# Other ranks, limits and planned durations for the list scheduler of a kernel with attention and a two-layer network

## The chip, the core and the metric

The kernel runs on one core of one Trainium2 chip. The metric is the time of one execution in microseconds (us) of the device. The engines of the core are called as in the profile: PE multiplies matrices (PEld loads its weights), DVE, ACT and POOL work on elements, and SP issues the loads and stores. Each engine takes its own instructions strictly in the order in which the program lists them; semaphores make one engine wait for another. PSUM, where PE writes, has 8 banks of 128 x 512 float32.

## The reference

The inputs are q, k and v of shape (8, 8, 576, 64) in float32 and two weight matrices, 512 x 2048 and 2048 x 512, which arrive as 8-byte floats. Keys and values are averaged over groups of 8 positions before the attention; its result is the input of a two-layer network with an activation made of softplus and erf.

```python
k_p = k.reshape(B, H, Sp, pool, D).mean(axis=3)
v_p = v.reshape(B, H, Sp, pool, D).mean(axis=3)
scores = scale * np.matmul(q, k_p.transpose(0, 1, 3, 2))
scores = scores - np.max(scores, axis=-1, keepdims=True)
attn = np.exp(scores)
attn = attn / (np.sum(attn, axis=-1, keepdims=True) + 1e-09)
x = np.matmul(attn, v_p)            # then heads side by side: 4608 tokens x 512
...
h = x @ w_in
sp = np.maximum(h, 0.0) + np.log1p(np.exp(-np.abs(h)))
g = h * erf(sp)
return (g @ w_out).astype(np.float32)
```

## The kernel before, in words

**Precision.** PE multiplies in a format with fewer bits than float32, so each operand is split into a high part and a remainder, and each product is made of three matmuls (high x high, low x high, high x low). That is why ACT (or POOL) casts, and DVE or POOL subtracts, after nearly every step.

**Chunks and steps.** The 4608 tokens are cut into 9 chunks (`ck`) of 512. For each chunk there are 16 steps (`ft`), one for each 128 columns of `w_in` and 128 rows of `w_out`: 144 steps `n` in all. The first product of a step (`gemm1`, L584) is 12 matmuls into one bank of kind `h`; the second (`gemm2`, L631) is 12 matmuls that add to four banks of kind `o`, which belong to the chunk until they are stored (L643 to L649). `pair(n)` takes two steps together: softplus (L602) and erf (L609) need different tables of ACT, loaded once each for a pair. Then come the product (L612), the cast `gh` (L614) and the remainder `gl` (L617). In chunk 0 (`kept` is false) the two `h` banks are held until the product is done; later the first product is copied out at once (L589, L590).

**Attention.** `job` treats a block of up to 256 tokens of one batch. A batch's first block loads the keys and values (L383), sums them over 8 positions (L386 on DVE for the first two batches, L389 to L393 on POOL for the others), and writes the split keys `kbd` (L402, L404) and values `vah`, `val`, `vb` (L412 to L425). `softmax_tile` treats 128 tokens: load and split q (L436 to L442), scores on PE (L476, in the wide form L452 and L454), the maximum (L481), in chunk 0 its scaling (L484), the exponentials on ACT (L491, L501), the sum, its guard (L505), the reciprocal (L507), the small product `bb` on POOL (L513), the normalisation (L517), transposes (L524, L531), and the split of the result (L528, L529, L536, L538, L541). Then PE multiplies with the values (L561), and ACT and DVE split the result into `xh` and `xl` (L565, L567), the input of `gemm1`. A chunk's `gemm1` needs all attention of that chunk.

**Weights.** There are 32 pieces (16 of each matrix), 512 KB each. `load_weights` loads one (L345) and turns its 8-byte floats into a high and a low part: two operations of ACT (L348, and L353 or on POOL L355), two of DVE (L357, L359), a cast on ACT or POOL (L309, L310) and a subtraction on POOL (L364). It uses one of the two buffers `f`, one of the three `hs`, and a bank of kind `cv`. All this happens once, in chunk 0.

**The order.** The program does not run in the order in which it is written. `op` records each operation with its engine, a planned duration, and a rank (`prio`, smaller is sooner) in units of steps: `gemm1` of step n has rank n, `gemm2` n + `G2`. `Program.order` then plays the whole kernel through with these durations and lists the operations. For each engine it takes, among the operations whose inputs are ready and whose rank is at most `window` above what PE has reached, the one with the smallest planned start plus `SLACK` nanoseconds for each unit of rank; of the engines' choices the earliest start goes first. An operation with two possible engines may go to its second one where that ends no more than `BIAS` later. `DELAY` is the planned time from one engine's end to another's start, `SAME` that within an engine, `DGE` and the start value of `free["SP"]` belong to the loads. `port` marks DVE operations that the plan keeps apart from POOL. The buffers of each kind, and the banks by kind (`CAP_H`, `CAP_O`, `CAP_ATT`, `CAP_CV`, eight together), limit what may be under way. Where PE is planned to be idle before `FILL` (57 us), fillers are put in (L675): matmuls on constants whose result nobody reads. The list is fixed when the program is built; at run time nothing is reordered.

The ranks that matter here: a weight piece has the rank `due` = ft + `W_IN`, or ft + `G2` + `W_OUT`; its load has `due` - `LEAD`, its conversion `due` - 3 to `due` - 2.4. The tiles of chunk 0 have `T0` + `T0_STEP` x (0 to 3); those of a later chunk 16 x (ck - 1) + 4 x t less `SHIFT` (or `B1` for chunk 1). Keys are summed at the rank of their batch's first tile plus `KEYS`, values at that plus `VALS`; a load stands one rank ahead of its sum. The values' matmuls come `VAL_R` after the last tile of the block.

## Time and profile before

| what | us |
|---|---|
| median of 3 runs | 950.01 (949.89 to 951.83) |
| the profiled execution, its own time | 949.92 |
| its span (first to last instruction) | 948.0 |
| PE busy in the span | 928.0 (98%) |
| ACT, DVE, POOL busy | 653.7, 531.9, 348.0 |
| all loads of weights, keys, values and q of chunks 0 and 1 | DMA above 0.8 busy until about 70 us |

The profile comes from one execution. A row of a timeline gives the start in us from the beginning of the span, the length, the engine, the line of the kernel, the operation, what it writes and reads, how many were merged, and in brackets the engine's idle time before it with what ended that. A row of a view by stretches gives the stretch, its length and the busy time (and number of instructions) of each engine in it. The end of a matmul is modelled, so neighbouring matmuls overlap in the rows; distances between starts are better read than lengths.

### The profile page before, as it was taken

How to read it: one execution, taken by the hardware profiler on the slowest of the kernel's cores; microseconds unless marked ns; L12 is line 12 of the kernel's file. 1: busy time of each engine (PE TensorE's matmuls, PEld its weight loads, DVE VectorE, ACT ScalarE, POOL GpSimd, SP SyncE). 2: the span in 40 equal slices, each digit the busy share in tenths (PEclk: the TensorE clock that was granted, in tenths of full speed). 3: DMA queues.
4: the chain of work that ended last, by engine and by line, in shares of the span. 5: the costliest groups of instructions: out<-in, count | busy, mean ns of one | idle time of the engine just before them, and what ended most of it. 6: DMA issues, size and time to landing. Idle time of an engine off the chain costs nothing.

```text
span 948.0 us, 13049 instructions
## 1 busy us (share of the span) xinstructions
PE 928.0 (98%) x4636; PEld 771.9 (81%) x4636; DVE 531.9 (56%) x1021; ACT 653.7 (69%) x1131; POOL 348.0 (37%) x451
## 2 busy tenths in 40 slices
PE   7899989999999999999999999999999999999998
PEld 6778868888888888888888888888888888888886
DVE  6978686755565454555565655655476446423232
ACT  4789985867676767766676667766676667656664
POOL 3689986243322354235321452234342111101000
PEclk9999999999999999999999999999999999999999
DMA  8990112212111121111110122002210010001001
GB/s 322 363 357 7 37 36 70 77 38 62 39 45 36 38 67 45 45 43 47 51 67 13 37 68 78 23 14 59 68 56 23 1 45 1 1 1 44 1 1 45
DMA packets 30352, 58.58 MB, mean 62 GB/s; under 512 B 7120, under 2 KB 7248, under 8 KB 30288
## 3 DMA queue, kind: packets, MB, share of 16 engines
q1 hardware_dynamic: 30000, 57.23, 18.1%
q8 instruction: 37, 0.61, 0.3%
q10 hardware_dynamic: 288, 0.52, 0.1%
q14 instruction: 27, 0.22, 0.1%
HBM read 48.30 MB, written 9.44 MB: 61 GB/s over the span
## 4 chain that ended last, share of the span: by engine, by line
PE 84%; DVE 1%; ACT 0%; POOL 0%; issue 0%; POOLq 0%
PE banks L631 38%; PE banks L584 37%; PE banks L561 4%; PE banks L452 2%; PE banks L524 1%; PE banks L454 1%; PE banks L476 1%; PE banks L531 0%; DVE kbd L404 0%; DVE z L503 0%; ACT L501 0%; DVE hs L612 0%; ACT y L602 0%; DVE z L505 0%; DVE s L517 0%; ACT s L501 0%
## 5 line engine op out<-in xcount | busy, mean ns | idle before, releaser
L584 PE MATMUL banks<-xh,wi 128*128 128x512 f32 x1152 | 381.2, 393 | 3.5 <-DVE y L612 2.8
L631 PE MATMUL banks<-wo,gh 128*128 128x512 f32 x1152 | 363.2, 396 | 0.8 <-DVE etl L529 0.7
L584 PEld LDWEIGHTS banks<-xh,wi 128*128 128x128 f32 x1152 | 217.1, 188 | 51.1 <-DVE y L612 4.4
L631 PEld LDWEIGHTS banks<-wo,gh 128*128 128x128 f32 x1152 | 207.5, 188 | 39.6 <-DVE etl L529 1.1
L631 PE MATMUL banks<-wo,gl 128*128 128x512 f32 x576 | 225.3, 391 | 0.0
L584 PE MATMUL banks<-xl,wi 128*128 128x512 f32 x576 | 225.1, 391 | 0.0
L617 DVE TENSOR_TENSOR gl<-hs,gh 128x512 fp32r<-128x512 f32 x73 | 53.6, 736 | 157.4 <-ACT gh L614 153.3
L617 POOL TENSOR_TENSOR gl<-hs,gh 128x512 fp32r<-128x512 f32 x55 | 71.4, 1298 | 175.2 <-ACT gh L614 174.6
L631 PEld LDWEIGHTS banks<-wo,gl 128*128 128x128 f32 x576 | 108.1, 188 | 24.2 <-DVE gl L617 0.4
L590 ACT COPY hs<-banks 128x512 f32<-128x512 f32 x56 | 32.8, 586 | 136.2 <-PE banks L584 133.3
L584 PEld LDWEIGHTS banks<-xl,wi 128*128 128x128 f32 x576 | 108.6, 188 | 21.8
L614 ACT CAST gh<-hs 128x512 fp32r<-128x512 f32 x128 | 78.4, 614 | 35.5 <-PE banks L631 31.3
L589 DVE COPY hs<-banks 128x512 f32<-128x512 f32 x72 | 49.8, 692 | 92.1 <-PE banks L584 91.7
L602 ACT ACT_TABLE_LOAD x72 | 92.4, 1283 | 3.0 <-DVE gl L617 1.8
L612 DVE TENSOR_TENSOR hs<-y,hs 128x512 f32<-128x512 f32 x128 | 84.1, 697 | 15.2 <-ACT y L609 15.1
L609 ACT ACT_TABLE_LOAD x68 | 87.2, 1283 | 1.2
L442 POOL TENSOR_TENSOR ql<-raw,qh 128x512 fp32r<-128x512 f32 (+1 forms) x36 | 44.4, 1232 | 106.4 <-ACT qh L309 106.2
L609 ACT ACTIVATE y<-y 128x1024 f32<-128x1024 f32 (+1 forms) x73 | 76.4, 1048 | 0.8
L389 POOL TENSOR_TENSOR raw<-raw 128x256 f32<-128x256 f32 (+1 forms) x60 | 50.9, 849 | 70.5 <-DMA raw<-vl 40.8
L602 ACT ACTIVATE y<-hs 128x512 f32<-128x512 f32 x128 | 73.8, 624 | 0.7
L541 POOL TENSOR_SCALAR etb<-etb 32x256 fp32r<-32x256 f32 (+1 forms) x40 | 18.3, 458 | 88.8 <-ACT etb L536 54.8
L501 ACT ACTIVATE s<-s,cst 128x576 f32<-128x576 f32 (+1 forms) x36 | 27.9, 775 | 30.3 <-DVE s L465 30.2
(100 smaller groups left out, 1194.4 us busy)
## 6 DMA issues: line engine op xcount, KB each, us to landing
raw<-vl SPq DMA_DIRECT2D x42, 256.0 KB, 2.7
out<-f SPq DMA_DIRECT2D x34, 256.0 KB, 2.0
raw<-kl SPq DMA_DIRECT2D x30, 288.0 KB, 2.8
wi<-wi SPq DMA_DIRECT2D x16, 512.0 KB, 6.8
wo<-wo SPq DMA_DIRECT2D x16, 512.0 KB, 6.8
raw<-qa SPq DMA_DIRECT2D x28, 256.0 KB, 2.6
hs<-qa SPq DMA_DIRECT2D x4, 256.0 KB, 5.1
raw<-qa SPq DMA_DIRECT2D x8, 128.0 KB, 2.5
```

Of the source, the lines that this page charges most:

```text
L389: op("POOL", gps(4 * size), prio, lambda: nc.gpsimd.tensor_add(t.ap[:, 0:4], t.ap[:, 0:4], t.ap[:, 4:8]), [t], [t])
L442: e.tensor_sub(ql.ap[:, :, :T], raw.ap[:, :, :T], f32(qh.ap[:, :, :T]))
L561: nc.tensor.matmul(d, w, e, start=(i == 0), stop=(i == 3), skip_group_check=True)
L584: nc.tensor.matmul(ph.ap, w_in[ft].ap[:, w, P * p:P * p + P], x.ap[:, p, :], start=(p == 0 and q == 0), stop=(p == NP - 1 and q == 2))
L589: op("DVE", dve(TC), n + u + 1.2, lambda u=u, ph=ph: nc.vector.tensor_copy(hs[u].ap, ph.ap), [ph], [hs[u]], alt=("ACT", act(TC, True), lam ...
L590: [ph], [hs[u]], alt=("ACT", act(TC, True), lambda u=u, ph=ph: nc.scalar.copy(hs[u].ap, ph.ap)))
L602: nc.scalar.activation(y.ap[:, half(k)], hh[k].ap, AF.Softplus)
L609: op("ACT", act(w), n + 1.9, lambda sl=sl: nc.scalar.activation(y.ap[:, sl], y.ap[:, sl], AF.Erf), own, own, funcs="sigmoid")
L612: op("DVE", dve(TC), n + 1.9, lambda k=k: nc.vector.tensor_mul(g(k), y.ap[:, half(k)], hh[k].ap), [(y, k), hh[k]], [gs[k]], port=kept)
L614: op("ACT", act(TC), n + 2.0, lambda k=k: nc.scalar.copy(gh[k].ap, g(k)), [gs[k]], [gh[k]])
L617: e.tensor_sub(gl[k].ap, g(k), f32(gh[k].ap))
L631: nc.tensor.matmul(o[t].ap, g.ap[:, gs], w_out[ft].ap[:, w], start=(ft == 0 and q == 0), stop=(ft == NJ - 1 and q == 2))
```

## The change

The scheduler's code is the same. Its numbers change: the ranks, window, slack and bias, the bank limits (six banks for attention in place of four), and the planned durations and delays of engines and loads; three short DVE operations (L484, L505, L507) are now marked `port`. The operations and their operands stay as they are.

```diff
--- before.py
+++ after.py
@@ -36,24 +36,24 @@
 NB = 2
 
 
-WINDOW = 10
-SHIFT = 4
+WINDOW = 8
+SHIFT = 3
 B1 = 2
-T0, T0_STEP = -10.5, 1.0
-VAL_R = 3.5
-KEYS, KEYS_R, KEYS_S = -5.5, 0.5, -1.0
-VALS, VALS_R, VALS_S = -2.0, 0.5, -1.2
+T0, T0_STEP = -10.5, 1.5
+VAL_R = 3.0
+KEYS, KEYS_R, KEYS_S = -9.0, 0.5, -1.0
+VALS, VALS_R, VALS_S = 0.0, 0.4, -1.2
 Q_DUE = 5.2
-W_IN, W_OUT = -1.0, -2.0
-LEAD = 9
-G2 = 5.0
+W_IN, W_OUT = 3.0, 1.0
+LEAD = 6
+G2 = 5.5
 ON_DVE = 2
-CAP_H, CAP_O, CAP_ATT, CAP_CV = 2, 4, 4, 2
+CAP_H, CAP_O, CAP_ATT, CAP_CV = 2, 4, 6, 2
 ON_ACT = (0,)
 WIDE_FROM = 2
-SLACK, BIAS = 30, 2000
+SLACK, BIAS = 80, 4000
 FILL, MARGIN = 57000.0, 300
-DGE = 1200
+DGE = 2000
 TURN = 0.0
 SWITCH = 1300
 C_ID = 0
@@ -129,8 +129,8 @@
 
 
 
-    DELAY = {"PE": 200, "ACT": 160, "DVE": 200, "POOL": 160, "SP": 900}
-    SAME = {"PE": 0, "ACT": 130, "DVE": 130, "POOL": 105, "SP": 0}
+    DELAY = {"PE": 200, "ACT": 220, "DVE": 260, "POOL": 160, "SP": 900}
+    SAME = {"PE": 0, "ACT": 190, "DVE": 190, "POOL": 105, "SP": 0}
 
     def __init__(self, capacity, window):
         self.ops, self.capacity, self.window, self.filler = [], capacity, window, None
@@ -172,7 +172,7 @@
 
     def order(self):
         free = {e: 0.0 for e in self.DELAY}
-        free["SP"] = 2150.0
+        free["SP"] = 2400.0
         slots = {t: [0.0] * n for t, n in self.capacity.items()}
         avail = {e: [] for e in free}
         for i, o in enumerate(self.ops):
@@ -291,13 +291,13 @@
 
 
     def act(n, psum=False):
-        return 0.84 * n + (160 if psum else 190)
+        return 0.84 * n + (90 if psum else 130)
 
     def dve(n):
-        return 1.15 * (n + 66) / 0.96
+        return 1.04 * n + 95
 
     def gps(n):
-        return 2.5 * n + 110
+        return 2.25 * n + 130
 
     def both(pool_too, cost, pool_cost, prio, fn, *access):
 
@@ -342,7 +342,7 @@
         if wide:
 
 
-            op("SP", 1350, due - LEAD, lambda: nc.sync.dma_start(raw.ap.rearrange("p f w -> p (f w)"), src), [], [raw])
+            op("SP", 1290, due - LEAD, lambda: nc.sync.dma_start(raw.ap.rearrange("p f w -> p (f w)"), src), [], [raw])
             b = bank("cv")
             bits = lambda: b.ap.bitcast(U32)
             op("ACT", act(n), due - 3, lambda: nc.scalar.activation(
@@ -350,9 +350,9 @@
 
             low = buf("hs", [n], U32)
             byte = lambda: raw.ap.bitcast(mybir.dt.uint8).rearrange("p f (w e) -> p f w e", w=2)[:, :, 0, 3]
-            op("ACT", act(n), due - 3, lambda: nc.scalar.activation(
+            op("ACT", act(n) + 130, due - 3, lambda: nc.scalar.activation(
                 low.ap, byte(), AF.Identity, bias=bias[1], scale=1 / 32), [raw], [low],
-               alt=("POOL", 0.833 * n + 161, lambda: nc.gpsimd.tensor_scalar(
+               alt=("POOL", 0.833 * n + 260, lambda: nc.gpsimd.tensor_scalar(
                    out=low.ap, in0=byte(), scalar1=1 / 32, scalar2=1 / 64 - 0.5, op0=ALU.mult, op1=ALU.add)))
             op("DVE", dve(n), due - 2.7, lambda: nc.vector.scalar_tensor_tensor(
                 bits(), bits(), 3, low.ap, ALU.logical_shift_left, ALU.bitwise_or), [b, low], [b])
@@ -380,7 +380,7 @@
 
             def load_pool(src, dst, p, size, prio, tag):
                 t = buf(tag, [size, POOL] if on_dve else [POOL, size])
-                op("SP", 10.3 * size, prio - 1, lambda: nc.sync.dma_start(
+                op("SP", (14.4 if first and p < NP and size == SP else 10.3) * size, prio - 1, lambda: nc.sync.dma_start(
                     t.ap, src.rearrange("(p a b) -> p a b", p=P, b=t.ap.shape[2])), [], [t])
                 if on_dve:
                     op("DVE", dve(8 * size), prio, lambda: nc.vector.tensor_reduce(
@@ -433,7 +433,7 @@
             wide_scores = T == P and ck >= WIDE_FROM
             raw, qh, ql = buf("hs" if first else "raw", [NP, P]), buf("qh", [NP, P], F32R), buf("ql", [NP, P], F32R)
             s, m, z, bb = buf("s", [H, SP]), buf("m", [H]), buf("z", [H]), buf("bb", [NP, 16])
-            op("SP", 5.2 * T, r - (Q_DUE if first else 2), lambda: nc.sync.dma_start(raw.ap[:, :, :T], 
+            op("SP", 5.2 * T + 400 * (first and at == 0), r - (Q_DUE if first else 2), lambda: nc.sync.dma_start(raw.ap[:, :, :T], 
                 qa[qo:qo + P * NP * T].rearrange("(p n t) -> p n t", p=P, n=NP)),
                [], [raw])
             copy(ck < 2, 4 * T, r - 0.6, lambda: qh.ap[:, :, :T], lambda: raw.ap[:, :, :T], [raw], [qh])
@@ -476,14 +476,14 @@
                             nc.tensor.matmul(o, q.ap[:, p, :T], kbd[:, p, 2 * SP * ko:2 * SP * ko + 2 * SP],
                                              start=(i == 0 and pp == 0), stop=(i == 2), skip_group_check=True)
 
-                op("PE", 6 * 107, r, scores, [qh, ql, KBD], [ps], [s, m, z])
+                op("PE", 6 * 111, r, scores, [qh, ql, KBD], [ps], [s, m, z])
                 gs = slice(4 * g, 4 * g + 4)
                 op("DVE", dve(4 * SP), r + 0.4, lambda pv=pv, gs=gs: nc.vector.tensor_reduce(
                     m.ap[:T, gs], pv(), AX.X, ALU.max), [ps], [(m, g)])
                 if on_act:
-                    op("DVE", dve(4), r + 0.5, lambda gs=gs: nc.vector.tensor_scalar(
+                    op("DVE", 150, r + 0.5, lambda gs=gs: nc.vector.tensor_scalar(
                         out=m.ap[:T, gs], in0=m.ap[:T, gs], scalar1=-1.0 / 64.0, scalar2=-EC,
-                        op0=ALU.mult, op1=ALU.add), [(m, g)], [(m, g)])
+                        op0=ALU.mult, op1=ALU.add), [(m, g)], [(m, g)], port=True)
 
                     def exps(ps=ps, g=g):
                         for i in range(4):
@@ -502,9 +502,9 @@
                     s.ap[:T], s.ap[:T], AF.Sigmoid, bias=bias[0][:T], scale=1.0 / 64.0), [s], [s], funcs="sigmoid")
                 op("DVE", dve(H * SP), r + 1.0, lambda: nc.vector.tensor_reduce(
                     z.ap[:T], s.ap[:T], AX.X, ALU.add), [s], [z])
-            op("DVE", dve(8), r + 1.0, lambda: nc.vector.tensor_scalar(
-                out=z.ap[:T], in0=z.ap[:T], scalar1=EPS, scalar2=None, op0=ALU.add), [z], [z])
-            op("DVE", dve(48), r + 1.0, lambda: nc.vector.reciprocal(z.ap[:T], z.ap[:T]), [z], [z])
+            op("DVE", 180, r + 1.0, lambda: nc.vector.tensor_scalar(
+                out=z.ap[:T], in0=z.ap[:T], scalar1=EPS, scalar2=None, op0=ALU.add), [z], [z], port=True)
+            op("DVE", dve(48), r + 1.0, lambda: nc.vector.reciprocal(z.ap[:T], z.ap[:T]), [z], [z], port=True)
 
 
             def ends():
@@ -514,7 +514,7 @@
 
             op("POOL", gps(64), r + 1.2, ends, [s, z], [bb])
 
-            both(ck < 2, dve(H * SP), gps(H * SP), r + 1.2, lambda e: e.tensor_mul(
+            both(ck < 2, dve(H * SP), 1170, r + 1.2, lambda e: e.tensor_mul(
                 s.ap[:T], s.ap[:T], z.ap[:T].unsqueeze(2).broadcast_to([T, H, SP])), [s, z], [s])
             pa, pb = bank("att"), bank("att")
 
```

## The prediction, made before the change was timed

> **What bounds the kernel now.** I read the page's head, then the busy time of the engines in six stretches, cut at points where PE's work changes.
>
> ```profile
> span 948.0 us, 13049 instructions
> ...
> 0.00:43.73 43.73, 35.05 (x280) 29.42 (x281) 33.86 (x77) 27.76 (x104) 24.30 (x37) 1.00 0.93 339
> 43.73:74.16 30.43, 28.29 (x174) 23.14 (x171) 23.28 (x50) 24.01 (x42) 23.41 (x27) 1.00 0.86 325
> 74.16:124.62 50.46, 49.95 (x244) 40.81 (x243) 37.51 (x67) 46.69 (x73) 46.80 (x53) 1.00 0.07 20
> 124.62:160.35 35.73, 31.21 (x146) 24.93 (x147) 28.33 (x49) 25.37 (x48) 26.65 (x36) 0.95 0.17 53
> ...
> 160.35:948.00 787.65, 783.47 (x3800) 1.00 0.13 39
> ```
>
> The columns are the stretch, its length, busy PE, PEld, DVE, ACT and POOL, then granted clock, DMA share and GB/s (the last row: PE alone). From 160.35 us on PE is busy for 783.47 of 787.65 us; the 4.2 us left are mostly the last eviction and store. A new order cannot win there; it can only lose. So the change is decided before 160 us, where chunk 0 runs. There the busy PE is partly fillers (matmuls of no use, L675) that the planner puts where it foresees idle time:
>
> ```profile
> 0.00:43.73 43.73, 22.68 (x168) 17.18 (x168) 1.00 0.93 339
> 43.73:74.16 30.43, 6.19 (x51) 4.47 (x48) 1.00 0.86 325
> ```
>
> Before 160 us PE thus wastes 22.68 us of fillers and 43.73 - 35.05 = 8.68 us of idle time ahead of the first matmul of the network (L584), then 6.19 + 2.14 us to 74.16, 0.51 us to 124.62, and 4.52 us to 160.35. The stretch from 74 to 125 has almost none, so PE keeps up well even while the weights are converted. I followed each loss back through the timelines of the engines.
>
> **First loss: chunk 0's attention is late.** These rows are of DVE, ACT and PE (start, length, what, idle time before it and its releaser).
>
> ```profile
> 12.90 0.81 DVE L481 TENSOR_REDUCE m<-banks 128x4 f32<-128x288 f32 x2
> ...
> 14.56 0.69 DVE L386 TENSOR_REDUCE vs<-gl 128x64 f32<-128x512 f32 x1 [0.84 <-DMA gl<-vl]
> 15.22 0.69 DVE L386 TENSOR_REDUCE vs<-gh 128x64 f32<-128x512 f32 x1
> 15.82 0.23 DVE L484 TENSOR_SCALAR m<-m 128x4 f32<-128x4 f32 x2
> ...
> 26.82 1.41 DVE L386 TENSOR_REDUCE ks<-raw 128x72 f32<-128x576 f32 x2
> 28.26 0.70 DVE L357 SCALAR_TENSOR_TENSOR banks<-banks,hs 128x512 uint32<-128x512 uint32 x1
> 28.87 0.45 DVE L481 TENSOR_REDUCE m<-banks 128x4 f32<-128x288 f32 x1
> ...
> 38.90 0.69 DVE L359 SCALAR_TENSOR_TENSOR f<-wi,banks 128x512 uint32<-128x512 uint32 x1
> ...
> 39.87 0.67 DVE L529 TENSOR_TENSOR etl<-banks,eth 128x512 fp32r<-128x512 f32 x1
> ```
>
> ```profile
> 30.94 0.32 ACT L491 ACTIVATE s<-banks,m 128x72 f32<-128x72 f32 x1 [1.82 <-DVE m L484]
> 38.19 0.59 ACT L528 CAST eth<-banks 128x512 fp32r<-128x512 f32 x1
> ```
>
> ```profile
> 27.30 0.39 PE L476 MATMUL banks<-kbd,qh 128*128 128x144 f32 x2
> 43.73 0.48 PE L584 MATMUL banks<-xh,wi 128*128 128x512 f32 x1
> ```
>
> The two maxima of tile 0 end at 13.71, but their scaling (L484) starts at 15.82, because DVE has two sums of values ahead of it and waits for their load: 2.1 us. Tile 3's scores are in the making at 27.30, and DVE takes its maximum at 28.87, after two sums of chunk 1's keys (1.41) and a weight operation (0.70); ACT idles 1.82 us for it. Tile 3's L528 ends at 38.78, L529 follows at 39.87: 1.1 us later, behind a weight operation and what stands after it.
>
> **Second loss: the first two pairs of network steps.** In chunk 0 a pair keeps both `h` banks until softplus, erf and product are done, so whatever ACT does in between delays the next pair.
>
> ```profile
> 51.37 1.09 ACT L602 ACTIVATE y<-banks 128x512 f32<-128x512 f32 x2
> 52.34 0.38 ACT L528 CAST eth<-banks 128x256 fp32r<-128x256 f32 x1
> 54.11 0.63 ACT L309 ACTIVATE wo<-f 128x512 fp32r<-128x512 f32 x1 [1.39 <-DVE f L359]
> 54.65 0.62 ACT L348 ACTIVATE banks<-wo 128x512 f32<-128x512 f32 x1
> 55.29 1.28 ACT L609 ACT_TABLE_LOAD   x1
> ...
> 64.26 0.63 ACT L309 ACTIVATE wi<-f 128x512 fp32r<-128x512 f32 x1 [2.20 <-DVE f L359]
> ...
> 67.97 1.28 ACT L602 ACT_TABLE_LOAD   x1
> ```
>
> ```profile
> 64.22 0.39 PE L584 MATMUL banks<-xh,wi 128*128 128x512 f32 x1
> ```
>
> Between softplus and erf of pair 0 ACT waits 1.39 us for a weight and does two weight operations: with them gone, erf's table load would follow softplus and one short copy at about 52.7 in place of 55.29, 2.6 us sooner. Pair 1's last first-product matmul starts at 64.22 and is through near 64.5, but its softplus starts at 67.97, behind weight operations like the one at 64.26 with its wait: up to 3.5 us.
>
> **Third loss: the end of chunk 0.**
>
> ```profile
> L505 DVE TENSOR_SCALAR z<-z x40: 152/172/3094, 19.6 to 808.4; 128x8 f32<-128x8 f32 x32, 64x8 f32<-64x8 f32 x8
> L507 DVE RECIPROCAL z<-z x40: 185/202/206, 20.1 to 808.6; 128x8 f32<-128x8 f32 x32, 64x8 f32<-64x8 f32 x8
> ```
>
> ```profile
> 130.28 3.09 DVE L505 TENSOR_SCALAR z<-z 64x8 f32<-64x8 f32 x1
> ```
>
> ```profile
> 136.59 1.28 ACT L602 ACT_TABLE_LOAD   x1 [1.79 <-DVE gl L617]
> ```
>
> ```profile
> 142.78 0.50 PE L584 MATMUL banks<-xh,wi 128*128 128x512 f32 x1 [2.32 <-DVE y L612]
> ...
> 143.35 0.76 PE L584 MATMUL banks<-xh,wi 128*128 128x512 f32 x2
> ...
> 147.70 0.62 PE L584 MATMUL banks<-xh,wi 128*128 128x512 f32 x2
> 148.39 0.62 PE L584 MATMUL banks<-xh,wi 128*128 128x512 f32 x2
> ```
>
> An operation of 0.17 us on eight columns took 3.09 us while POOL ran back to back. DVE's queue is in order, so all behind it is late: the softplus at 136.59, and PE at 142.78 after 2.32 us of idle time. Then the clock halves: 12 matmuls from 143.35 to 147.70 take 4.35 us, where three take 0.69 us a little later (147.70 to 148.39), so 4.35 - 2.76 = 1.6 us more.
>
> **The change part by part.** No instruction is added or removed apart from fillers; the edits change what the planner believes (durations, delays, a loader that starts later, `port`) and what it prefers (ranks, window, slack, bank limits). Sums are against the profiled execution: 949.92 us, 1.96 us more than its span of 947.96; the median of the runs is 950.01.
>
> *Loads and attention over weights.* Weights load and convert 4 ranks (w_in) and 3.5 (w_out) later in rank, the loads 7 and 6.5, and a rank weighs 80 ns, not 30. Tile 3 (rank -7.5) led the first w_in conversion (-4) by 3.5 ranks or 105 ns, less than one operation of 0.6 us; now -6 stands against 0, 480 ns. From the first loss I count 2.1 us (the planner now believes the first loads slower, so it will not place the sums before they land), 0.7 of the weight ahead of the maximum, 1.1 at L529, and about as much again, 1.6, in the small waits that I didn't list: -5.5 us at the first matmul of the network (L584). Keys go the other way: their rank rises by 3.5, so the sums of chunk 1's keys (1.41 for two) stay ahead of tile 3, and I credit nothing for them. Bounds: -9 (all 8.68 us of PE's idle time there) and 0.
>
> *Weights behind the activation.* A w_in conversion had rank n - 4 beside the activation's n - 0.5 of the pair before it; now it has n. That takes 2.6 us out of pair 0 and up to 3.5 out of pair 1, of 8.33 us lost in that stretch. What is late next is the weight itself. I take -4, with bounds -6.1 and +3 (each of the two pairs waits for one late conversion on POOL, below).
>
> *Port and exact durations.* L484, L505 and L507 are now kept apart from POOL in the plan, and DVE, ACT and POOL have nearer durations. The 3.09 us wait and what follows are worth up to 2.32 + 1.6 = 3.9 of the 4.52 us plus 1.6; a new order will have other collisions. I take -2.5, bounds -3.9 and +3.9 (the same stall once more). Keeping L507 apart can hold a reciprocal for one POOL operation (1.29 us, the row below) in a softmax; it is inside the +3.9. The Trainium skill, "SBUF — State Buffer" (its part on the two sides of SBUF), says that the port pair that VectorE and GpSimd share is an exclusive lock for a whole instruction, for two-port modes or two SBUF inputs; L505's longest agrees, while the reciprocal, 185 to 206 ns over its 40 instances, never shows it, so by that rule a third of this edit buys nothing, and up to 4 x 1.29 us on chunk 0's path would be lost: 945.6 us.
>
> *Conversions displaced.* All this moves conversions later:
>
> ```profile
> L364 POOL TENSOR_TENSOR wi<-f,wi x16: 1263/1290/1396, 32.7 to 128.4; 128x512 fp32r<-128x512 f32 x16
> L364 POOL TENSOR_TENSOR wo<-f,wo x16: 1279/1300/1727, 54.8 to 150.2; 128x512 fp32r<-128x512 f32 x16
> ```
>
> Their last step runs until 129.7 for w_in, whose last piece is first used after 142.78: a lead of 13 us, so POOL's queue may slip that far before PE waits. But POOL and ACT are busy 93% from 74 to 125, so part of what is gained at the start is paid back there: +2.5, between 0 and +5.5 (the whole gain of the start).
>
> *Loads of 512 KB at 1290 ns* instead of 1350: no weight at risk.
>
> ```profile
> 60.00:70.00 10.00, 8.40 (x45) 6.54 (x44) 7.19 (x19) 7.39 (x17) 9.75 (x11) 1.00 1.03 408
> ```
>
> At 408 GB/s one takes 524288/408 = 1285 ns, as planned. The Trainium skill, "DMA: Bandwidth & Descriptors" (Specifications), puts HBM at about 358 GB/s for a core, by which it would be 1.46 us and the last of 32 pieces 5.6 us later than planned, the sum at most 946.0 us; the trace disagrees, and decides.
>
> *Six attention banks, window 8, G2, SHIFT, VAL_R.* Four `o` and two `h` banks leave two for attention once the second products run, so the limit matters only before. In the steady part the order changes a little: 0, with +5 as the bad end (a held-back PE for at most 8 ranks x 80 ns = 0.64 us at each of 8 changes of chunk).
>
> Sum: -5.5 - 4 - 2.5 + 2.5 = -9.5; 949.92 - 9.5 = **940.4 us**.
>
> **Rivals.** *Weights too late (slower).* Ranked at their step's own rank, conversions lose their stock; the 13 us lead is two steps, and the rank moves by four. Once it is zero, each pair waits for its two pieces on POOL, 2 x 1.29 us, and a stall over 2 us halves the clock as above, 1.6 us. For the last four pairs of chunk 0 that is 4 x 4.2 = 17 us, less the 9.5 + 2.5 won elsewhere: 950 + 5 = 955 us. For it: POOL's 93%. Against it: the lead, and greedy engines that convert whenever they idle. It decides from the pair at which PE first waits for L364.
>
> *Given back whole.* ACT, DVE and POOL have the same work, and if they bound chunk 0, an earlier start only makes PE wait later: 949.5 us. For it: their 93%. Against it: DVE's 37.51 of 50.46 us, and POOL's 24.30 of 43.73 at the start.
>
> *All of it.* Each loss goes at its better bound short of the start's (-5.5 - 6.1 - 3.9) and nothing is paid back: 949.92 - 15.5 = 934.4 us. For it: each loss has one plain cause that the edits address. Against it: a new order makes new collisions.
>
> **Chances and range.** Forecast 0.58 (its own range 935 to 946), all of it 0.14, given back whole 0.12, weights too late 0.16. A difference under 0.2%, 1.9 us, cannot be told from none here. Faster is the forecast, all of it and a quarter of the gain given back: 0.75; same is half of that one, 0.06; slower is its last quarter and the late weights, 0.19. The range that leaves about a fifth outside: 932 to 953 us.
>
> **What would show it.** The first matmul of the network (L584) at about 38 us; no weight operation on ACT between the softplus and erf of the first pairs; L505 without instances of several us before 160 us; the first matmul of chunk 1 (160.35 now) at about 151; the stretch behind it still without idle time on PE. Wrong would be PE waiting for L364 or L309 in chunk 0, a first matmul still beyond 42 us, or new waits behind chunk 0.

## The result, and the profile after

The changed kernel takes 943.40 us (median of 4 runs, 942.97 to 944.21); the kernel before, run beside it, 950.92 us. The ratio is 0.9918, with a 95% interval of 0.9894 to 0.9941: faster by 0.8%, 7.5 us, where 9.5 had been forecast. The profiled execution took 942.97 us.

Below are the head of the profile after and the busy time of the engines in five stretches (columns as before: stretch, length, PE, PEld, DVE, ACT, POOL, granted clock, DMA share, GB/s). They are cut at the same points of the work as before: the first matmul of the network, those of the third and of the seventh pair, and that of chunk 1.

```profile
span 940.9 us, 13043 instructions
...
0.00:42.33 42.33, 36.86 (x307) 32.04 (x308) 32.88 (x76) 26.88 (x103) 23.38 (x36) 1.00 0.96 350
42.33:69.20 26.87, 25.06 (x150) 20.88 (x150) 22.65 (x47) 20.37 (x36) 20.90 (x26) 1.00 0.94 356
69.20:122.70 53.50, 49.66 (x238) 39.41 (x236) 40.88 (x72) 46.88 (x73) 47.76 (x57) 1.00 0.12 36
122.70:150.00 27.30, 26.33 (x132) 21.25 (x130) 21.73 (x40) 24.34 (x43) 24.61 (x27) 1.00 0.11 32
150.00:940.90 790.90, 787.02 (x3822) 656.32 (x3820) 432.89 (x823) 543.79 (x891) 174.31 (x262) 1.00 0.13 40
```

And the fillers (L675) in the first two of them, PE and PEld:

```profile
0.00:42.33 42.33, 23.63 (x183) 18.26 (x183) 1.00 0.96 350
42.33:69.20 26.87, 4.50 (x37) 3.53 (x37) 1.00 0.94 356
```

A stretch can also get shorter because work was moved out of it. So what PE loses is the better measure: its idle time (length less busy time), plus its fillers, plus the time at half clock. The numbers of before come from the rows in the prediction.

| stretch, ending at | before: idle + fillers + half clock | after | difference |
|---|---|---|---|
| first matmul of the network | 8.68 + 22.68 | 5.47 + 23.63 | -2.3 |
| third pair | 2.14 + 6.19 | 1.81 + 4.50 | -2.0 |
| seventh pair | 0.51 | 3.84 | +3.3 |
| first matmul of chunk 1 | 4.52 + 1.6 | 0.97 | -5.1 |
| the end | 4.18 | 3.88 | -0.3 |

That is -6.4 of the 7.1 us by which the span is shorter; the other 0.7 is spread over PE's busy time, whose ends are modelled. Four of the prediction's five signs came: no weight operation between softplus and erf of the first pairs, no L505 of several us, chunk 1 at 149.97 (forecast about 151), no new idle time behind it. One did not: the first matmul of the network starts at 42.33, where about 38 was forecast and "beyond 42" was named as wrong. Another sign that was named as wrong came too: PE waits for L364 in chunk 0 (below).

**The start.** First ACT before, then ACT after: where the exponentials of tiles 0 and 1 begin (in the second fence also tile 3, and its L528).

```profile
16.02 0.32 ACT L491 ACTIVATE s<-banks,m 128x72 f32<-128x72 f32 x1 [2.48 <-DVE m L484]
...
18.40 0.36 ACT L491 ACTIVATE s<-banks,m 128x72 f32<-128x72 f32 x1
```

```profile
12.46 0.32 ACT L491 ACTIVATE s<-banks,m 128x72 f32<-128x72 f32 x1
...
19.45 0.32 ACT L491 ACTIVATE s<-banks,m 128x72 f32<-128x72 f32 x1
...
29.79 0.38 ACT L491 ACTIVATE s<-banks,m 128x72 f32<-128x72 f32 x1
...
37.49 0.58 ACT L528 CAST eth<-banks 128x512 fp32r<-128x512 f32 x1
```

Tile 0 is 3.56 us earlier, more than the 2.1 that was credited. Tile 1 is 1.05 us later than before. Tile 3 is 1.15 us earlier (30.94 before), its L528 0.7 us (38.19 before). The gain of tile 0 was thus gone one tile later. DVE after shows how (the row behind the dots is tile 0's normalisation, L517):

```profile
15.35 0.69 DVE L386 TENSOR_REDUCE vs<-gl 128x64 f32<-128x512 f32 x1 [0.98 <-DMA gl<-vl]
15.96 0.45 DVE L481 TENSOR_REDUCE m<-banks 128x4 f32<-128x288 f32 x1
16.32 0.94 DVE L505 TENSOR_SCALAR z<-z 128x8 f32<-128x8 f32 x1
17.18 0.45 DVE L481 TENSOR_REDUCE m<-banks 128x4 f32<-128x288 f32 x1
17.55 0.67 DVE L386 TENSOR_REDUCE vs<-gh 128x64 f32<-128x512 f32 x1
18.14 0.74 DVE L386 TENSOR_REDUCE ks<-raw 128x72 f32<-128x576 f32 x1
18.80 0.47 DVE L414 SCALAR_TENSOR_TENSOR val<-vs,cst,vah 128x256 fp32r<-128x256 f32 x1
19.19 0.19 DVE L507 RECIPROCAL z<-z 128x8 f32<-128x8 f32 x1
19.30 0.18 DVE L484 TENSOR_SCALAR m<-m 128x4 f32<-128x4 f32 x2
...
20.06 0.76 DVE L517 TENSOR_TENSOR s<-s,z 128x576 f32<-128x576 f32 x1 [0.18 <-POOL bb L513]
```

Before, two sums of values and their load stood ahead of tile 0's scaling. Now a sum of values that waits 0.98 us for its load stands ahead of tile 1's maxima, and two sums, a split and a reciprocal stand between those (ended at 17.63) and their scaling at 19.30. DVE has the same work to do; the order chose another tile to wait for it. Tile 0 keeps little of its lead as well. Its guard L505 starts at 16.32, but its reciprocal L507 stands behind a maximum, two sums and a split, at 19.19, and so its normalisation starts at 20.06, only 0.71 us sooner than before:

```profile
20.77 0.76 DVE L517 TENSOR_TENSOR s<-s,z 128x576 f32<-128x576 f32 x1 [0.48 <-POOL bb L513]
```

Tile 3 then waits on PE, in order behind tile 1 (before, then after):

```profile
24.76 0.66 PE L524 MATMUL banks<-cst,s 128*128 128x128 f32 x4
...
25.83 0.43 PE L476 MATMUL banks<-kbd,qh 128*128 128x144 f32 x2
```

```profile
26.39 0.63 PE L524 MATMUL banks<-cst,s 128*128 128x128 f32 x4 [0.32 <-DVE m L484]
26.77 0.43 PE L476 MATMUL banks<-kbd,qh 128*128 128x144 f32 x2
```

The first matmul of tile 3's scores stands behind tile 1's transposes (L524) in both orders. The transposes start 1.63 us later than before, and the scores 0.94 us later, at 26.77.

**The pairs.** ACT after, in the first two pairs:

```profile
49.60 1.09 ACT L602 ACTIVATE y<-banks 128x512 f32<-128x512 f32 x2
50.57 0.38 ACT L528 CAST eth<-banks 128x256 fp32r<-128x256 f32 x1
50.97 1.28 ACT L609 ACT_TABLE_LOAD   x1
...
63.82 1.08 ACT L602 ACTIVATE y<-banks 128x512 f32<-128x512 f32 x2
65.04 0.42 ACT L309 ACTIVATE vb<-f 128x256 fp32r<-128x256 f32 x1
65.48 1.28 ACT L609 ACT_TABLE_LOAD   x1
```

From the start of softplus to the table of erf it is now 1.37 us in pair 0 (3.92 before, 51.37 to 55.29), with no weight operation between.

**What came instead.** PE's waits after, from 40 to 160 us (total, times, longest), and the first of the kind that the slower rival named:

```profile
PE banks L631 <- POOL wo L364: 1.9, 3, 1.1
PE banks L584 <- DVE f L359: 1.2, 1, 1.2
```

```profile
78.83 0.50 PE L631 MATMUL banks<-wo,gh 128*128 128x512 f32 x1 [0.24 <-POOL wo L364]
```

Before, PE waited for no L364. Now it waits three times, 1.9 us together, and once for a conversion's L359: the conversions were moved later, and 3.3 us of the gain is paid back in that stretch.

### The profile page after: what moved, and what is told of

It is laid out like the page before. It is cut to its first block, busy times and chain, and to the rows that moved or that the text cites. A ratio compares the mean times of both kernels' runs of the same rounds, so it can differ in the third digit from the quotient of the medians.

```text
span 940.9 us, 13043 instructions
## 1 busy us (share of the span) xinstructions
PE 924.9 (98%) x4640; PEld 769.9 (82%) x4640; DVE 551.0 (59%) x1055; ACT 662.3 (70%) x1144; POOL 291.0 (31%) x404
## 4 chain that ended last, share of the span: by engine, by line
PE 84%; DVE 0%; ACT 0%; issue 0%
PE banks L631 39%; PE banks L584 37%; PE banks L561 4%; PE banks L452 2%; PE banks L524 1%; PE banks L454 1%; PE banks L476 1%; PE banks L531 0%; DVE f L359 0%; DVE banks L357 0%; ACT gh L643 0%; DVE kbd L404 0%
## 5 line engine op out<-in xcount | busy, mean ns | idle before, releaser
L617 DVE TENSOR_TENSOR gl<-hs,gh 128x512 fp32r<-128x512 f32 x122 | 84.3, 691 | 156.5 <-ACT gh L614 146.5
L442 POOL TENSOR_TENSOR ql<-raw,qh 128x512 fp32r<-128x512 f32 (+1 forms) x36 | 47.6, 1322 | 244.7 <-ACT qh L309 240.3
L612 DVE TENSOR_TENSOR hs<-y,hs 128x512 f32<-128x512 f32 x128 | 99.6, 819 | 8.0 <-ACT y L609 7.6
L389 POOL TENSOR_TENSOR raw<-raw 128x256 f32<-128x256 f32 (+1 forms) x60 | 48.5, 810 | 57.6 <-DMA raw<-kl 28.8
L460 DVE TENSOR_TENSOR s<-s,banks 128x144 f32<-128x144 f32 x100 | 25.9, 299 | 50.9 <-ACT s L458 50.7
L567 DVE TENSOR_TENSOR xl<-banks,xh 128x256 fp32r<-128x256 f32 (+3 forms) x96 | 32.7, 352 | 21.2 <-ACT xh L565 20.3
L536 ACT CAST etb<-banks 32x128 fp32r<-32x128 f32 (+1 forms) x80 | 19.4, 243 | 35.3 <-PE banks L531 34.8
```

The lines of the kernel that those rows point to most:

```text
L389: op("POOL", gps(4 * size), prio, lambda: nc.gpsimd.tensor_add(t.ap[:, 0:4], t.ap[:, 0:4], t.ap[:, 4:8]), [t], [t])
L442: e.tensor_sub(ql.ap[:, :, :T], raw.ap[:, :, :T], f32(qh.ap[:, :, :T]))
L567: op("DVE", dve(n), r + 0.5, lambda p=p, pv=pv: nc.vector.tensor_sub(xl.ap[:, p, xs], pv.ap[:, :n], f32(xh.ap[:, p, xs])), [pv, (xh, (p, o ...
L612: op("DVE", dve(TC), n + 1.9, lambda k=k: nc.vector.tensor_mul(g(k), y.ap[:, half(k)], hh[k].ap), [(y, k), hh[k]], [gs[k]], port=kept)
L617: e.tensor_sub(gl[k].ap, g(k), f32(gh[k].ap))
```

## The experiments

Each line: the median, the ratio to the kernel before on the same chip with its 95% interval, and the start of the first matmul of the network (before 43.73, after 42.33) in the profiled execution. A number that is taken back reshuffles the whole list, and each row is one order. Already small edits move the span of the profiled execution by about 1.5 us either way: 939.3 us with the keys and 942.4 with the delays as before, beside 940.9. So a row says what that order does, and less surely what its number means.

| kernel | us | ratio | first matmul |
|---|---|---|---|
| the change | 943.40 | 0.9918 (0.9894 to 0.9941) | 42.33 |
| ranks and limits alone | 946.80 | 0.9955 (0.9939 to 0.9970) | 40.46 |
| durations, delays, ports alone | 947.43 | 0.9958 (0.9943 to 0.9973) | 48.0 |
| weights ranked as before | 950.50 | 0.9995 (0.9986 to 1.0004) | 50.29 |
| before, with only the weights' ranks | 952.81 | 1.0008 (0.9989 to 1.0026) | 44.7 |
| keys as before | 942.81 | 0.9910 (0.9890 to 0.9930) | 42.55 |
| no `port` marks | 943.22 | 0.9921 (0.9901 to 0.9941) | 44.60 |
| loads' times as before | 946.59 | 0.9947 (0.9929 to 0.9965) | 47.34 |
| delays as before | 944.68 | 0.9933 (0.9918 to 0.9947) | 47.52 |
| eight-position sums of batch 1 cut | 943.87 | 0.9929 (0.9914 to 0.9944) | 41.92 |
| four attention banks | 945.62 | 0.9947 (0.9932 to 0.9961) | 42.1 |
| other ranks, a | 938.92 | 0.9872 (0.9855 to 0.9889) | 42.4 |
| other ranks, b | 937.98 | 0.9868 (0.9853 to 0.9883) | 41.2 |

### Which half of the change it is

One kernel has before's durations, delays, load times and no marks, with the change's ranks, window, slack and limits; the other is its mirror image. First the former.

```diff
-    DELAY = {"PE": 200, "ACT": 220, "DVE": 260, "POOL": 160, "SP": 900}
+    DELAY = {"PE": 200, "ACT": 160, "DVE": 200, "POOL": 160, "SP": 900}
...
-        return 1.04 * n + 95
+        return 1.15 * (n + 66) / 0.96
```

> The changed kernel with the durations, delays and port marks of before; ranks, window, slack and bank limits as changed (the constants ahead of the scheduler). If the gain of 7 us came from the ranks (weights behind attention and behind the activation): 942 to 945 us, PE's second pair starts within 14.6 us of the first (14.5 in the changed kernel, 15.1 before). If it needed the durations: 948 to 952 us, with DVE again waiting for loads that the plan believes landed (first network matmul after 43 us) and L505 again waiting more than 2 us for POOL before 160 us.

```diff
-W_IN, W_OUT = 3.0, 1.0
-LEAD = 6
+W_IN, W_OUT = -1.0, -2.0
+LEAD = 9
...
-SLACK, BIAS = 80, 4000
+SLACK, BIAS = 30, 2000
```

> The changed kernel with the ranks, window, slack and bank limits of before; durations, delays and port marks as changed. If the durations made the gain: 942 to 946 us and no L505 over 1 us before 160 us. If the ranks made it: 948 us or more; by the ranks before, weights go ahead of chunk 0's attention by one operation at a time, so the first network matmul stays at 43 to 46 us.

In the medians each half wins about 0.4%, and 0.9955 x 0.9958 = 0.9913 is the whole within its interval. So neither half is the whole cause alone, and neither time fits one of the two outcomes that had been set out for it. L505 takes at most 1.26 us with the ranks alone and 1.30 us with the durations alone, so either half is rid of the stall of 3.09 us. With the durations alone the first matmul comes at 48.0, later than the 43 to 46 that either theory allowed. The ranks alone bring the earliest start of all, 40.46, in an execution of 943.44 us, the fastest of its six: it was granted the full clock, the other five (946.49 to 947.74 us) 0.994 to 0.998. So in that execution the ranks alone come within 0.5 us of the change, and the median's other half goes with a lower clock whose causes those executions, without a trace, do not show. A start 1.9 us sooner than the change's wins nothing over it.

### The weights' ranks

```diff
-W_IN, W_OUT = 3.0, 1.0
-LEAD = 6
+W_IN, W_OUT = -1.0, -2.5
+LEAD = 9
```

> The changed kernel with the weights' ranks as before (conversions at n - 4 and n, loads 7 and 6.5 ranks sooner), all else as changed. Theory: ranking the weights below attention and activation is the part that wins. By it this kernel loses most of the gain, 947 to 952 us; the first network matmul comes at 46 to 50 us (42.3 in the changed kernel), and weight operations stand on ACT between softplus and erf of pair 0 again (pairs 0 to 1 over 15 us apart). Rival (any new order does as well): 943 +- 2 us.

Measured 0.9995: the whole gain is gone, as the theory had it, and the first matmul is late (50.29, where it said 46 to 50). Two other signs did not come: the second pair starts 10.6 us behind the first (60.93), not over 15, and no weight operation stands between softplus and erf of pair 0. Its stretches up to the first matmul and from there to the third pair, and its waits of PE from 40 to 160 us:

```profile
0.00:50.29 50.29, 44.53 (x365) 37.98 (x366) 40.53 (x89) 34.39 (x116) 29.73 (x42) 1.00 0.99 363
50.29:75.80 25.51, 22.73 (x108) 18.93 (x106) 22.80 (x46) 21.72 (x38) 19.64 (x23) 0.87 0.68 253
```

```profile
PE banks L531 <- DVE f L359: 2.8, 1, 2.8
PE banks L584 <- DVE y L612: 2.4, 1, 2.4
```

With the weights first, the network starts 8 us later than in the change, and waits of over 2 us with a reduced clock (0.87) return. But the first two pairs take 25.5 us, not more than the 26.9 of the change: ACT and POOL did more conversions before the start (34.39 and 29.73 us busy ahead of it, against 26.88 and 23.38). So a short stretch of the pairs does not prove that the rank of the weights made it short. This order also has a long stall of its own, although L505 is marked here:

```profile
106.77 3.96 DVE L505 TENSOR_SCALAR z<-z 128x8 f32<-128x8 f32 x1
```

Its granted clock before 160 us is 0.96 in the mean, against 1.00 in the change, which is about 0.04 x 160 = 6.4 us of PE's time.

(With `G2` half a step higher than in the kernel before, -2.5 is the same rank for `w_out` as -2.0 there.) The opposite question is whether these three numbers alone would do it in the kernel before:

```diff
-W_IN, W_OUT = -1.0, -2.0
-LEAD = 9
+W_IN, W_OUT = 3.0, 1.5
+LEAD = 6
```

> The kernel before with the weights' ranks alone as changed (conversions at n and n + 3.5, loads 7 and 6.5 ranks later); slack, durations and all else as before. With the weights' old ranks the changed kernel had lost its whole gain. If the weights' ranks are enough by themselves: 944 to 947 us, and no weight operation on ACT between softplus and erf of pair 0. If they need the larger slack and the corrected durations: 949 to 952 us, with PE's stalls moved and not gone.

Measured 1.0008, no difference. Its longest wait of PE from 40 to 160 us (total, times, longest):

```profile
PE banks L584 <- DVE y L612: 3.5, 2, 2.8
```

The long wait for L612 in the later part of chunk 0, 2.3 us at the longest before, is still there. No weight operation stands on ACT between softplus and erf of pair 0 here either, and yet nothing is won. So without these ranks the change loses its gain, and with them alone the kernel before gains nothing.

### Why the first matmul moved so little

Four theories named what holds the chain of chunk 0: the keys, which the change ranks up; the marks, which keep DVE off POOL; the planned loads or delays; and DVE's own queue, with chunk 1's sums in it.

```diff
-KEYS, KEYS_R, KEYS_S = -9.0, 0.5, -1.0
+KEYS, KEYS_R, KEYS_S = -5.5, 0.5, -1.0
```

> The changed kernel with KEYS at -5.5 as before. First theory on why the first network matmul came at 42.3 us and not at 38: the sums of chunk 1's keys (four of 0.74 us on DVE between 13.6 and 23.2 us) stand in the way of chunk 0's softmax. By it the first network matmul comes about 2 us sooner, at 40 to 40.5 us, and the kernel is 0 to 2 us faster than the changed one. Rival: the port mark on the reciprocal costs it; then the first network matmul stays at 42 +- 0.7 us and the time within 2 us of 943.4.

The first matmul stays (42.55) and the time is the same within its interval: not the keys.

```diff
-                        op0=ALU.mult, op1=ALU.add), [(m, g)], [(m, g)], port=True)
+                        op0=ALU.mult, op1=ALU.add), [(m, g)], [(m, g)])
...
-                out=z.ap[:T], in0=z.ap[:T], scalar1=EPS, scalar2=None, op0=ALU.add), [z], [z], port=True)
-            op("DVE", dve(48), r + 1.0, lambda: nc.vector.reciprocal(z.ap[:T], z.ap[:T]), [z], [z], port=True)
+                out=z.ap[:T], in0=z.ap[:T], scalar1=EPS, scalar2=None, op0=ALU.add), [z], [z])
+            op("DVE", dve(48), r + 1.0, lambda: nc.vector.reciprocal(z.ap[:T], z.ap[:T]), [z], [z])
```

> The changed kernel without the three new port marks (L484, L505, L507). Theory of the port: in the changed kernel the reciprocal L507 starts 2.9, 0.9, 1.2 and 1.8 us after the start of its L505 in chunk 0's four tiles, because the plan keeps it off POOL and puts sums between; without the marks it follows at once and the first network matmul comes 2 to 4 us sooner (38.5 to 40.5 us), but L505 waits for POOL again, over 2 us at least once before 160 us; 943 to 948 us in all. Rival (the marks do nothing for the chip): 943 +- 1 us and the first network matmul at 42.3.

The first matmul is 2.3 us later and the time is the same: the marks neither hold the start back nor bring a gain that this can measure. L505 over the whole execution (count, then shortest, median and longest in ns), without the marks and then with them:

```profile
L505 DVE TENSOR_SCALAR z<-z x40: 153/166/1256, 16.3 to 806.8; 128x8 f32<-128x8 f32 x32, 64x8 f32<-64x8 f32 x8
```

```profile
L505 DVE TENSOR_SCALAR z<-z x40: 153/164/1254, 16.3 to 806.4; 128x8 f32<-128x8 f32 x32, 64x8 f32<-64x8 f32 x8
```

The longest is 1.25 us in both, 3.09 before. The long stall went without the marks as well, and it came with them, 3.96 us, where the weights are ranked as before. It belongs to single orders, not to the marks.

```diff
-DGE = 2000
+DGE = 1200
...
-        free["SP"] = 2400.0
+        free["SP"] = 2150.0
...
-            op("SP", 1290, due - LEAD, lambda: nc.sync.dma_start(...
+            op("SP", 1350, due - LEAD, lambda: nc.sync.dma_start(...
```

(and the first keys and q of chunk 0 at their old rates)

> The changed kernel with the planned times of the loads as before (loader free at 2150, DGE 1200, weights 1350, keys and q without their extra). Theory: with the loads planned too early, DVE and POOL are again put behind loads that haven't landed (in the kernel before 2.2 and 5.1 us between 40 and 60 us), so the first network matmul comes within 1 us of 43.5, and the time is 945 to 948 us. Rival, from ranks alone with old durations giving a first matmul at 40.5: the longer planned loads are what moved the start later; then it comes at 40 to 41.3 us and the time is 942 +- 1.5 us.

```diff
-    DELAY = {"PE": 200, "ACT": 220, "DVE": 260, "POOL": 160, "SP": 900}
-    SAME = {"PE": 0, "ACT": 190, "DVE": 190, "POOL": 105, "SP": 0}
+    DELAY = {"PE": 200, "ACT": 160, "DVE": 200, "POOL": 160, "SP": 900}
+    SAME = {"PE": 0, "ACT": 130, "DVE": 130, "POOL": 105, "SP": 0}
```

> The changed kernel with the planned delays between operations as before (DELAY of ACT and DVE 60 ns shorter, SAME 60 ns shorter). Theory: the longer planned delays moved the start later, since the plan then fills each step of the softmax chain with other work; by it the first network matmul comes at 40 to 41.3 us here. Rival: it stays at 42.3 +- 0.7 us, and the delays only help later, where the time loses 1 to 3 us (944 to 946).

Both start the network 5 us later (47.34 and 47.52), outside what theory and rival had allowed, so neither old number would have brought the start forward. With the loads as before, the time is 3.2 us longer than the change's in the medians, and the intervals overlap a little. With the delays as before it is 1.3 us longer, within the intervals. That a start 5.2 us later goes with a loss of 1.3 us hints how little the start counts by itself:

```profile
0.00:160.00 160.00, 147.60 (x869) 1.00 0.49 175
```

```profile
0.00:160.00 160.00, 29.97 (x224) 1.00 0.49 175
```

These are PE's busy time before 160 us with the old delays, and the fillers in it: 117.6 us of useful work. For the change they are:

```profile
0.00:160.00 160.00, 147.92 (x876) 1.00 0.49 174
```

```profile
0.00:160.00 160.00, 28.13 (x220) 1.00 0.49 174
```

119.8 us, 2.2 more. More than half of the 5.2 us at the start was made up before 160 us.

For DVE's queue, the ten sums of chunk 1's batch (L386) were shortened: only the first of the eight positions is copied, so this kernel leaves out seven of eight positions of the keys and values of batch 1. The order is the change's.

```diff
-                    op("DVE", dve(8 * size), prio, lambda: nc.vector.tensor_reduce(
-                        dst.ap[:, p, :], t.ap, AX.X, ALU.add), [t], [(dst, p)])
+                    op("DVE", dve(8 * size), prio, (lambda: nc.vector.tensor_copy(
+                        dst.ap[:, p, :], t.ap[:, :, 0])) if b else (lambda: nc.vector.tensor_reduce(
+                        dst.ap[:, p, :], t.ap, AX.X, ALU.add)), [t], [(dst, p)])
```

> The changed kernel in the very same order, but it leaves out a part: of batch 1's ten sums on DVE (keys and values over 8 positions) only the first of the 8 positions is copied, about 0.15 us in place of 0.67 to 0.74 us. Five of these stand on DVE ahead of the first network matmul. Theory: that matmul is set by DVE's queue, which is busy with 24 us for chunk 0 and 8.7 us of other work out of 38; then it comes 2 to 2.7 us sooner, at 39.6 to 40.3 us. Rival: the chain of waits through ACT, PE and POOL sets it, and DVE's work lies in its gaps; then it stays at 42.3 +- 0.5 us. If more speed on DVE also counts in the rest of chunk 0, the time is 940 to 942 us, else 943 +- 1.

The first matmul moves by 0.4 us (41.92). The test is weak: of the four copies of keys ahead of it, two took 1.03 and 0.75 us, no less than the sums. DVE in that kernel (its lines are one higher), and POOL at that time:

```profile
17.17 1.03 DVE L386 COPY ks<-raw 128x72 f32<-128x72 f32 x1
...
19.01 0.18 DVE L485 TENSOR_SCALAR m<-m 128x4 f32<-128x4 f32 x2
```

```profile
16.85 1.28 POOL L443 TENSOR_TENSOR ql<-hs,qh 128x512 fp32r<-128x512 f32 x1 [2.26 <-ACT qh L309]
```

The copy of 72 elements ends at 18.20, as POOL's operation does at 18.13. So the scaling of tile 1 starts at 19.01, hardly earlier than 19.30. No single cause of the missing 4 us was found. What the traces of before and after show is that the wait is handed on from tile to tile.

### Six banks for attention

```diff
-CAP_H, CAP_O, CAP_ATT, CAP_CV = 2, 4, 6, 2
+CAP_H, CAP_O, CAP_ATT, CAP_CV = 2, 4, 4, 2
```

> The changed kernel with four banks for attention as before. The prediction's zero for this edit: 943.4 +- 1.5 us, first network matmul at 42.3 +- 1 us. Rival (six banks let chunk 0's attention run further ahead): first matmul 2 us later or more, 945 us or more.

Measured 0.9947, against 0.9918 with six. The medians are 2.2 us apart and the intervals overlap. The first matmul stays at 42.1; the time lies where the rival had it, the start where the zero had it. PE's longest wait from 40 to 160 us is new:

```profile
PE banks L561 <- DVE etl L529: 2.6, 1, 2.6
```

The banks are probably worth about 2 us in this setting, where the prediction had put nothing; it is not settled.

### A better order

If the change is a matter of preferences among orders, other numbers should do better. Two sets were taken for which the planner's own clock ends earlier. The larger differences of the first from the change:

```diff
-WINDOW = 8
+WINDOW = 12
...
-T0, T0_STEP = -10.5, 1.5
+T0, T0_STEP = -9.5, 1.25
...
-W_IN, W_OUT = 3.0, 1.0
-LEAD = 6
+W_IN, W_OUT = 3.0, 0.5
+LEAD = 5
```

> The changed kernel with other ranks, chosen for the shortest plan (928.0 us in the plan's own clock, 932.4 for the changed kernel, 934.9 for the one before): T0 -9.5 and 1.25, VAL_R 2.5, KEYS_R 0.4, KEYS_S 0.75, VALS_R 0.3, VALS_S -0.8, Q_DUE 4.2, W_OUT 0.5, LEAD 5, G2 5.75, WINDOW 12. If the corrected durations make the plan a guide to the chip: 937 to 941 us, first network matmul at 40 to 42 us. If the plan is no guide at this scale: 943 +- 2 us.

The second:

```diff
-WINDOW = 8
-SHIFT = 3
-B1 = 2
-T0, T0_STEP = -10.5, 1.5
-VAL_R = 3.0
-KEYS, KEYS_R, KEYS_S = -9.0, 0.5, -1.0
-VALS, VALS_R, VALS_S = 0.0, 0.4, -1.2
-Q_DUE = 5.2
-W_IN, W_OUT = 3.0, 1.0
-LEAD = 6
-G2 = 5.5
+WINDOW = 18.5
+SHIFT = -0.75
+B1 = 2.5
+T0, T0_STEP = -10.75, 0.875
+VAL_R = 3.875
+KEYS, KEYS_R, KEYS_S = -7.0, 0.95, -3.5
+VALS, VALS_R, VALS_S = -0.25, 0.8, -1.2
+Q_DUE = 2.2
+W_IN, W_OUT = 2.5, 0.25
+LEAD = 7.5
+G2 = 5.75
...
-SLACK, BIAS = 80, 4000
+SLACK, BIAS = 85.0, 4000
```

> As search_a from another start: WINDOW 18.5, SHIFT -0.75, B1 2.5, T0 -10.75 and 0.875, VAL_R 3.875, KEYS -7, 0.95, -3.5, VALS -0.25, 0.8, Q_DUE 2.2, W_IN 2.5, W_OUT 0.25, LEAD 7.5, G2 5.75, SLACK 85; 927.3 us in the plan's own clock. If the plan is a guide: 937 to 941 us; if not: 943 +- 2 us, or slower where an attention that is planned so late (SHIFT -0.75) leaves PE waiting at the changes of chunk, which the stretch behind 160 us would show.

Measured 938.92 us (0.9872) and 937.98 us (0.9868, 0.9853 to 0.9883). Both beat the kernel before and the change; the second is the fastest kernel here. The plan was a guide: its own times for the kernel before, the change and these two, 934.9, 932.4, 928.0 and 927.3 us, stand in the same order as the measured ones. (The profile of the first is of its slowest execution, 942.05 us.) The second's busy PE before and behind 160 us, and its fillers before:

```profile
0.00:160.00 160.00, 150.32 (x848) 1.00 0.48 173
160.00:936.20 776.20, 771.96 (x3756) 1.00 0.13 40
```

```profile
0.00:160.00 160.00, 24.82 (x183) 1.00 0.48 173
```

Before 160 us PE now does 150.32 - 24.82 = 125.5 us of useful work, 5.7 more than the change; the span is 940.9 - 936.2 = 4.7 us shorter. Behind 160 us its idle time is 4.2 us, as in the kernel before. Its first matmul starts only 1.1 us sooner than the change's. By the same two rows the kernel before comes to 144.14 - 28.87 = 115.3 us of such work, of which about 1.7 us were lost to a reduced clock. It is the useful work before 160 us that goes with the time. With the time lost to a reduced clock taken off (one minus the granted clock, summed over steps of 5 us), this work and the span add up to between 1057 and 1062 us in all 14 profiled executions, while the spans alone differ by 15 us; behind 160 us PE is idle for 3.8 to 4.5 us in each. The start shows no such tie: 40.46 us goes with a span of 941.7, 42.55 (keys as before) with 939.3, 47.52 with 942.4. This says where the time is won, not why one order packs more work into those 160 us than another.

## Why the prediction was right, and where it was not

**The bound: right.** "From 160.35 us on ... a new order cannot win there." Behind chunk 0 the idle time of PE is 4.18 us before, 3.88 after, 4.2 in the fastest kernel. Nearly every difference lies ahead of it. The sign "chunk 1 at about 151" came partly by luck: it had taken the whole gain as a shift of that point, but the point moved by 10.4 us and the span by 7.1, because 3.55 us of PE's work (787.02 us behind it, 783.47 before) moved behind it.

**Loads and attention over weights, -5.5: the step that failed.** Measured is -1.4 us at the first matmul, -2.3 by what PE loses. In this setting the direction of the ranks was right: with the weights ranked as before the first matmul goes to 50.29. (Put alone into the kernel before, the new ranks moved it from 43.73 to 44.7.) The single wait also went, and tile 0's exponentials came 3.56 us sooner. What failed was adding up 2.1 + 0.7 + 1.1 + 1.6, as if each wait removed moved the end of the chain by its length. Four tiles share DVE, ACT and PE, each in order; the work that stood before tile 0's scaling stands before tile 0's reciprocal and tile 1's scaling in the new order, and tile 3's scores, behind tile 1's transposes as before, come later with these. That is what the trace shows; why this order and no better one came out, no single experiment settles.

**Weights behind the activation, -4: sign seen, size halved, the ranks not needed for it.** The stretch is 3.6 us shorter, but PE's useful work in it also fell, from 28.29 - 6.19 = 22.1 to 25.06 - 4.50 = 20.6 us, so the loss shrank by 2.0. The weight operations between softplus and erf of pair 0 are gone, as forecast. But they are also gone with the weights ranked as before, and with all ranks as before and only the durations, delays and marks of the change. So the new ranks are not needed for it; they stood there in the order of before, and other orders do not have them. The kernel with the old weight ranks also has a stretch just as short.

**Port and exact durations, -2.5: more came, for another reason.** At the end of chunk 0 the loss went from 6.1 to 0.97 us: -5.1. The step had taken off part of the stall for "other collisions", and none came. Its reason, the marks, falls: without them neither the stall nor any of the time comes back, and with them another order stalls for 3.96 us. The mention of "SBUF — State Buffer" in the Trainium skill (the two sides of SBUF) had set the price of marking the reciprocal at up to 4 x 1.29 us. Without its mark the reciprocal is still never long:

```profile
L507 DVE RECIPROCAL z<-z x40: 183/196/205, 16.7 to 806.9; 128x8 f32<-128x8 f32 x32, 64x8 f32<-64x8 f32 x8
```

The page does not name the reciprocal; the trace agrees with its rule as the prediction applied it. But taking the three marks away won nothing, so the price was not paid.

**Conversions displaced, +2.5: right.** +3.3 us from 69 to 123 us, 1.9 of it in waits for L364 and 1.2 in one for L359. That with the old delays a start 5.2 us later goes with a loss of 1.3 us fits this.

**Loads at 1290 ns: the rate did not hold, the price of zero is open.** From 60 to 70 us the change moves

```profile
60.00:70.00 10.00, 10.00 (x52) 8.51 (x51) 9.55 (x16) 9.80 (x16) 9.41 (x10) 1.00 0.99 381
```

381 GB/s, after 408 before, so one load takes 524288/381 = 1376 ns there, more than the 1290 planned and the 1350 of the old plan. The prediction had taken a single stretch of 10 us for the rate. The profiled execution of 942.97 us stays below the 946.0 at most that the rule of 358 GB/s gave. That rule, from "DMA: Bandwidth & Descriptors" of the Trainium skill (Specifications), is a share of two busy cores by the same page's section Bandwidth, which gives more to a core whose neighbour is idle; both rates agree with that. The old load times as a whole cost 3.2 us in the medians; the single one of 1290 was not tried.

**Six banks, 0: probably wrong by 2 us.** The step said that the limit matters only until the second products run, and put no price on that time. With four banks the second pair starts at 58.8 us, with six at 56.8, after starts of the first that are alike (42.1 and 42.33).

**The rivals.** *Weights too late* had its place right and its size wrong: PE waits for L364 first at 78.83, and in all 1.9 us, not 17; the clock stays at 1.00. The lead of 13 us had been worked out for `w_in`; all three waits are for pieces of `w_out`. "It decides from the pair at which PE first waits for L364" was too strong. *Given back whole* is out: 3.3 us came back. *All of it*, 934.4 us, was not reached here; the fastest kernel's 937.98 shows that more of it can be had than the change took.

For the profiled execution 940.4 us was 2.6 us too low: the start fell short by 3.2 (by PE's loss), the pairs by 2.0, the pay-back was 0.8 more; the end of chunk 0 gave 2.6 more, the rest 0.9 (rounded). The total came close partly because these errors cancel.

## What to carry to other kernels

Waits that are removed one by one along a chain must not be added up when the waiting work shares in-order engines: move one instruction, then ask which one stands behind the moved work next. The start of a phase is a poor measure of a schedule; count the useful work of the bounding engine (busy time less fillers) up to the point from which it runs without a gap. Ranks and planned durations act together, so a constant tried alone in an old setting says little about its worth in the new one. And every such constant reshuffles the whole order, so one order with it and one without it do not tell its meaning from the luck of the draw.

## What the runs showed of the hardware that was not expected

A copy on DVE can be held beside POOL, not only L505: the copy of 72 elements took 1.03 us, from 17.17 to 18.20, beside POOL's L443 that ended at 18.13. That is one reason why the cut sums saved so little, and I had not expected it when I chose the copy. The Trainium skill, "SBUF — State Buffer" (Who interferes with whom), names copies and `tensor_scalar` among the operations that can contend with GpSimd, and says that `tensor_reduce` on trn2 never does. The trace agrees as far as these rows go: the sums of L386 took 0.67 to 0.75 us each in the change, none of them longer. That the copy waits for POOL is read from ends that coincide; it was not tested by itself.

A mark in the plan does not keep two operations apart on the chip: L505 took 0.94 us in the change (16.32 to 17.26), though marked, beside a POOL operation of 1.27 us that began at 15.96. The two long stalls lasted longer than any one operation of POOL. With the weights ranked as before, POOL's rows from 106.35 on follow each other without a gap until this one ends at 110.71, and POOL's next starts at 112.61:

```profile
109.42 1.29 POOL L364 TENSOR_TENSOR wo<-f,wo 128x512 fp32r<-128x512 f32 x1
```

The L505 there ran from 106.77 to 110.73. In the kernel before, the one from 130.28 ended at 133.37, and the first gap in POOL's rows lies between 133.35 and 133.43. In both, the short operation came through at POOL's first gap. That is read from two coincidences of times, and no run tested it. The plan is made of durations, and the engines run as their semaphores let them.
